# Windowed attention and a gated MLP on one core: order from a list scheduler, one stock of PSUM banks, casting loads for batches 0 and 1, DMA transposes for the later q and k

## Chip, cores, metric

One core of one Trainium2 chip. The metric is device time in microseconds (us) of one execution, median of several. "Span" is the profiled part of it, some 1.7 us shorter. TensorE is PE, VectorE DVE, ScalarE ACT, GpSimd POOL, SyncE SP in the profile. SBUF and PSUM are the memories that the kernels place their tiles in; every matmul of both kernels writes to one of PSUM's banks. The DMAs of the program are issued by GpSimd or SP, and the profile shows what the core's DMA engines move; a DMA has landed when its data is there.

## The reference

```python
# q, k, v: [8 batches, 8 heads, 576, 64]; float32
rel = pos[:, None] - pos[None, :]
plain   = (rel >= 0) & (rel < 32)                       # heads 0 to 3
dilated = (rel >= 0) & (rel < 128) & (rel % 4 == 0)     # heads 4 to 7
attn = softmax(where(mask, q @ k.T / 8, -1e9)) @ v
x = attn.transpose(0, 2, 1, 3).reshape(4608, 512)
h = x @ w_in                                            # [512, 2048]
out = (h * sigmoid(beta * h)) @ w_out                   # [2048, 512]
```

The MLP runs in nine tiles of 512 tokens, each with 16 groups of h (four matmuls of 512 columns each). Attention of one batch (576 tokens) is spread between the MLP's matmuls of the tile before.

## The kernel before

Its order is written by hand, and each engine carries out its own queue in that order (in the trace GpSimd's cast of batch 0's v at 23.0 us, then the loads of w_in from 25.0). Three pools share eight PSUM banks (2 + 1 + 5). q and k of the plain heads are loaded as float32, cast on an engine and transposed on TensorE; those of the dilated heads are cast into DRAM and loaded by DMA transposes.

```python
psum_h = psum("psum_h", 2)
psum_o = psum("psum_o", 1)
psum_at = psum("psum_at", 5)
# ...
cast_v(0, 1, G)                # G is GpSimd: waits for batch 0's v
for g in range(4):
    load_w_in(g)               # DMAs issued on GpSimd's queue, behind that cast
load_qk(1, "k")
load_qk(1, "q")
load_vd(1)
for name in STEPS_FIRST:       # "K0 Q0 K1 S00 Q1 ...": a fixed list of attention steps
    # ...
    attention_step(0, name)
for kind, hp in (("k", 0), ("q", 0), ("k", 1), ("q", 1)):
    cast_qk(1, kind, hp, G)
for g in range(4):
    load_w_out(g)
load_vp(1)
# ...
for t in range(NTT):           # then h and o groups of tile t, attention steps dealt between them
```

The softmax here doesn't subtract the row's maximum and nothing guards it: scores larger than these inputs give would overflow.

## Time and profile before

| | before |
|---|---|
| time, median (range) | 364.0 us (362.6 to 364.74, 4 runs) |
| span of the profiled run, mean granted clock | 364.4 us, 0.983 |
| first MLP matmul | 36.75 us |
| wait for batch 2's transposed q | 76 to 86 us |
| steady period | 36.0 us |

The prediction below quotes the views. The row of the granted TensorE clock, in tenths, 40 slices of the span:

```profile
PEclk9999999999996999999999999999999999999998
```

Only one slice (109 to 118 us, at 6 tenths) is well below full clock. The packed trace's first clock record in this run is at 41.6 us, and before it the row shows full clock, though the 512-column matmuls from 36.75 to 41.7 us start 0.427 us apart, for 0.216 from 150 us on: there the spacing of the matmuls is the surer sign.

A milestone that I use is the start of VectorE's gate, the instruction that writes g: there are 16 per tile (32 for tile 0 in the changed kernel, which cuts that tile in two), so a steady period is the time from one gate to the sixteenth after it. For the kernel before that is 258.5 - 222.5 = 36.0 us.

### The profile page before, as it was taken

The numbers are of one execution on the slowest core, as the hardware profiler recorded it, in microseconds if no ns is written. First come the engines' busy times: TensorE is split into PE (matmuls) and PEld (weight loads), VectorE is DVE, ScalarE is ACT, GpSimd is POOL, SyncE is SP. The second block draws the span as 40 slices with busy tenths as digits, with TensorE's granted clock in tenths as the row PEclk, the third lists the DMA queues.
The fourth block names the chain that finished last, engine by engine and source line by source line (L and its number), as shares of the span: only waits on it lengthen the run. The fifth ranks groups of instructions, "written<-read, shape, count | busy, mean of one in ns | idle before, by whom it ended". The sixth has DMA issues, their size and how long they took to land.

```text
span 364.4 us, 6201 instructions
## 1 busy us (share of the span) xinstructions
PE 315.1 (86%) x2305; PEld 167.3 (46%) x2305; DVE 205.2 (56%) x440; ACT 197.1 (54%) x380; POOL 149.8 (41%) x204
## 2 busy tenths in 40 slices
PE   0266999885977999989999999899989999999995
PEld 0254455442443555545554545454545444444442
DVE  6477488556641966485648565756576635334400
ACT  1373486354651776567656755575657545435511
POOL 8444740364285438453936493549243200000000
PEclk9999999999996999999999999999999999999998
DMA  7999999898937950983099419831101110111032
GB/s 180 167 242 210 221 205 149 216 219 216 221 76 188 232 81 23 215 222 78 29 220 250 93 33 233 221 82 30 31 29 31 29 31 29 42 47 29 29 75 72
DMA packets 66751, 45.77 MB, mean 126 GB/s; under 512 B 45968, under 2 KB 57248, under 8 KB 66464
## 3 DMA queue, kind: packets, MB, share of 16 engines
q1 hardware_dynamic: 55728, 35.67, 40.8%
q0 software_dynamic: 10992, 9.70, 17.0%
q8 instruction: 18, 0.29, 0.4%
q14 instruction: 13, 0.11, 0.1%
HBM read 40.89 MB, written 14.16 MB: 151 GB/s over the span
## 4 chain that ended last, share of the span: by engine, by line
PE 67%; DMA 10%; DVE 7%; POOL 6%; ACT 4%; issue 3%; SPq 2%; POOLq 0%; ACTq 0%
PE o_ps L376 28%; PE h_ps L345 26%; DMA w_in_bf<-in_moe_w_in_dram 3%; POOL pt L292 3%; DVE qzd L199 3%; PE at L345 3%; DMA qdT<-qd 3%; PE at L306 3%; SPq L192 2%; PE at L288 2%; DMA vd_st<-in_v_dram 2%; DVE g L353 2%; PE h_ps L376 2%; PE at L322 2%; POOL qb L206 2%
## 5 line engine op out<-in xcount | busy, mean ns | idle before, releaser
L353 DVE SCALAR_TENSOR_TENSOR g<-tnh,h_ps 128x512 bf16<-128x512 bf16 x134 | 91.3, 686 | 105.6 <-ACT tnh L350 105.2
L345 PE MATMUL h_ps<-xT,w_in_bf 128*128 128x512 bf16 x536 | 138.4, 384 | 12.0 <-DVE g L353 9.7
L376 PE MATMUL o_ps<-w_out_bf,g 128*128 128x512 bf16 x544 | 139.2, 384 | 2.9 <-ACT osb L381 2.9
L350 ACT ACTIVATE tnh<-h_ps,beta_half 128x512 bf16<-128x512 f32 x134 | 92.1, 687 | 69.6 <-PE h_ps L345 67.2
L345 PEld LDWEIGHTS <-w_in_bf 128*128 128x128 bf16 x576 | 52.7, 99 | 60.4 <-issue 15.7
L376 PEld LDWEIGHTS <-g 128*128 128x128 bf16 x576 | 52.6, 99 | 53.0 <-issue 6.1
L290 ACT ACTIVATE pt<-at 128x288 bf16<-128x288 f32 (+1 forms) x112 | 47.2, 443 | 11.9 <-PE at L288 11.9
L292 POOL TENSOR_TENSOR pt<-pt,mask_d 128x288 bf16<-128x288 bf16 x48 | 34.9, 727 | 41.0 <-ACT pt L290 35.1
L313 DVE TENSOR_TENSOR xs<-at,rcp 72x256 bf16<-72x256 f32 (+1 forms) x96 | 44.6, 465 | 3.3
L306 PEld LDWEIGHTS <-pt 128*128 128x128 bf16 x448 | 26.3, 103 | 20.4 <-POOL pt L292 8.0
L381 ACT ACTIVATE osb<-o_ps 128x512 f32<-128x512 f32 x34 | 20.3, 597 | 27.2 <-PE o_ps L376 27.2
L292 POOL TENSOR_TENSOR pt<-pt,mask_PP 128x384 bf16<-128x384 bf16 x24 | 22.3, 936 | 21.5 <-ACT pt L290 21.4
L332 ACT COPY xT<-at 128x288 bf16<-128x288 bf16 x32 | 12.7, 397 | 26.0 <-PE at L322 26.0
L322 PE MATMUL at<-ident_b,xs 72*128 72x72 bf16 (+1 forms) x224 | 21.6, 209 | 5.7 <-DVE xs L313 5.7
L292 POOL TENSOR_TENSOR pt<-pt,mask_FP 128x384 bf16<-128x384 bf16 x12 | 12.0, 998 | 35.2 <-ACT pt L290 35.2
L309 DVE RECIPROCAL rcp<-at 72x4 f32<-72x4 f32 (+1 forms) x96 | 17.1, 178 | 15.6 <-PE at L306 14.8
L306 PE MATMUL at<-vd,pt 128*128 128x65 bf16 x256 | 19.9, 201 | 6.8 <-POOL pt L292 6.8
L206 POOL CAST kb<-k_st 72x512 bf16<-72x512 f32 x28 | 16.3, 610 | 17.9 <-PE at L306 17.9
L322 PEld LDWEIGHTS <-xs 72*128 72x128 bf16 (+1 forms) x224 | 15.5, 101 | 17.2 <-DVE xs L313 7.7
L239 POOL CAST vd<-vd_st 128x2048 bf16<-128x2048 f32 x8 | 15.3, 1914 | 10.5 <-DMA vd_st<-in_v_dram 10.5
L288 PE MATMUL at<-qzd,kdT 128*128 128x144 bf16 x128 | 18.6, 238 | 0.7 <-DVE qzd L199 0.7
L206 POOL CAST qb<-q_st 72x512 bf16<-72x512 f32 x28 | 16.3, 610 | 4.8 <-DMA q_st<-in_q_dram 4.8
(64 smaller groups left out, 229.0 us busy)
## 6 DMA issues: line engine op xcount, KB each, us to landing
vp_st<-in_v_dram SPq DMA_DIRECT2D x24, 192.0 KB, 6.7
vd_st<-in_v_dram SPq DMA_DIRECT2D x8, 512.0 KB
k_st<-in_k_dram SPq DMA_DIRECT2D x6, 576.0 KB
q_st<-in_q_dram SPq DMA_DIRECT2D x6, 576.0 KB
vd_st<-in_v_dram SPq DMA_DIRECT2D x8, 384.0 KB
kd<-in_k_dram POOLq DMA_DIRECT2D x8, 288.0 KB, 7.7
qd<-in_q_dram POOLq DMA_DIRECT2D x8, 288.0 KB, 8.7
w_in_bf<-in_moe_w_in_dram POOLq DMA_DIRECT2D x4, 512.0 KB, 16.1
```

The lines of the kernel that those rows point to most:

```text
L206: (eng.copy if eng is nc.scalar else eng.tensor_copy)(out=qkb[b, kind][:, hp, :, h2, :], in_=stage[b, kind][:, 2 * hp + h2].rearrange("p ( ...
L288: nc.tensor.matmul(sc[:, a, 0:2 * n], lhsT=lhsT, rhs=rhs, start=True, stop=True)
L290: nc.scalar.activation(out=w, in_=sc[:, :, 0:2 * n], func=ACT.Exp, scale=SCALE)
L292: eng.tensor_tensor(out=w, in0=w, in1=mask, op=ALU.mult)
L306: nc.tensor.matmul(pv[:, a, h2, :], lhsT=pt[x][:, c:c + P], rhs=rhs, start=True, stop=True)
L313: nc.vector.tensor_tensor(out=xs_t[b, x, jx][:, a0:a0 + m], in0=pv[0:n, :, :, 0:D], in1=rcp[0:n, 0:m].unsqueeze(3).to_broadcast([n, m, 2, ...
L322: nc.tensor.transpose(xp[:, a * n:(a + 1) * n], xs[:, a].rearrange("p h d -> p (h d)"), ident_b[0:n, 0:n])
L345: nc.tensor.matmul(hps, lhsT=w_in_bf[:, kt, fb * P:(fb + 1) * P], rhs=xT[:, kt, t * NTOK:(t + 1) * NTOK], start=(kt == 0), stop=(kt == NKT ...
L350: nc.scalar.activation(out=tnh[:], in_=hps, func=ACT.Tanh, scale=beta_half[:, fb:fb + 1])
L353: nc.vector.scalar_tensor_tensor(out=g[:], in0=tnh[:], scalar=1.0, in1=hps, op0=ALU.add, op1=ALU.mult)
L376: nc.tensor.matmul(ops[:], lhsT=g_t[t, fb][:, tb * P:(tb + 1) * P], rhs=w_out_bf[:, fb, :], start=(fb == 0), stop=(fb == NFB - 1))
L381: nc.scalar.mul(out=osb[:], in_=ops[:], mul=0.5)
```

## The change

The intent: let a scheduler with estimated durations place every instruction, give all uses one stock of banks, start the MLP sooner, and take q/k transposes off TensorE from batch 2 on. The diff is long; its core, cut:

```diff
-    psum_h = psum("psum_h", 2)
-    psum_o = psum("psum_o", 1)
-    psum_at = psum("psum_at", 5)
+    BANKS = [psum_pool.tile([P, 512], FP32, name=f"bank{i}") for i in range(8)]
+    plan = Plan(range(8))                 # CAPS = {"h": 3, "o": 2, "a": 8}
...
-STEPS = ("K0 Q0 K1 Q1 S00 S01 ...").split()
+class Plan:                               # picks, again and again, the ready instruction that can
+    def run(self, filler=None, ...):      # start first, then by its place in the order (vt)
...
+    def direct_qk(b, z, h0, deps, vt):    # batches 0 and 1: casting load, token-major
+        src = (k, q)[z][b, h0:h0 + 4].rearrange("h (t T) d -> t h (T d)", T=R)
+        return load("POOL", ((ks, qs)[z][:, h0:h0 + 4], src), deps, vt, 576, .38)
+    def cast(b, z, h0, deps, vt): ...     # batches 2 to 7: cast into DRAM on GpSimd's queue,
+    def crossbar(b, z, h0, deps, vt): ... # then a DMA transpose on SP's, for all heads
...
+    def t_masks3(e):                      # late fills, one entry of GpSimd's queue
+        for n in ("FP", "PP"):
+            nc.gpsimd.tensor_copy(out=mask_e[n]..., in_=mask_p[n]...)
+        nc.gpsimd.memset(kz[:], 0.0)
+        nc.gpsimd.memset(qzd[1][64:128, 0], 0.0)
+        nc.gpsimd.memset(qzd[1][0:64, 1], 0.0)
...
-            nc.sync.dma_start(out=dst, in_=osb[a:a + n])     # rows scattered
+                nc.sync.dma_start(out=out[r0:r0 + P, cols], in_=ob[:, cols])
```

## The prediction

> **What bounds the kernel now.** I read the page's slices first, then the chain that ended last, then the instructions in order of time at the start and in one steady batch, then busy times by stretch.
>
> Slices of 9.1 us each (busy tenths):
>
> ```profile
> PE   0266999885977999989999999899989999999995
> DMA  7999999898937950983099419831101110111032
> ```
>
> The DMA row is full for ten slices (91 us) and falls off afterwards; the matmul row is full from the fifth slice on, with holes at slices 8 to 13. So there are two stages: a start bound by transfers, then a long stage bound by TensorE. The chain that ended last, from 0 to 40 us:
>
> ```profile
> 1.31 5.62 DMA kd<-in_k_dram
> 6.95 2.84 SPq L192
> 9.84 4.56 SPq L192
> 15.08 7.78 DMA vd_st<-in_v_dram
> 23.02 1.97 POOL vd L239
> 24.99 11.71 DMA w_in_bf<-in_moe_w_in_dram
> 36.75 1.89 PE h_ps L345 x4
> ```
>
> The first MLP matmul waits for w_in, and w_in is late because its issue stands on GpSimd's queue behind the cast of vd, which waits for a load that stands behind two DMA transposes on SP's queue. It is a serial chain of issues, not lack of bandwidth. The four matmuls from 36.75 start 0.42 us apart (38.43 - 36.75 over 4), against 0.215 later, so TensorE also starts at half speed, until 41.7: 12 matmuls, 2.5 us lost. One steady batch, in order of time:
>
> ```profile
> 249.93 1.03 PE L345 MATMUL h_ps<-xT,w_in_bf 128*128 128x512 bf16 x4
> 250.79 0.29 PE L288 MATMUL at<-qzd,kdT 128*128 128x144 bf16 x2
> 250.92 1.03 PE L376 MATMUL o_ps<-w_out_bf,g 128*128 128x512 bf16 x4
> ...
> 257.59 0.42 PE L253 MATMUL at<-ident_b,kb 72*128 72x72 bf16 x8
> 257.85 1.03 PE L345 MATMUL h_ps<-xT,w_in_bf 128*128 128x512 bf16 x4
> ...
> 267.14 0.38 PE L345 MATMUL h_ps<-xT,w_in_bf 128*128 128x512 bf16 x1 [1.45 <-DVE g L353]
> ```
>
> Starts, not durations, give the cost: four 512-column matmuls take 0.86 us (250.79 - 249.93), two 144-column ones 0.13, eight 72-column transposes 0.26. All fit columns/2.4 ns plus 2.5 ns. The last line is one of the two waits of the period (h has only two banks and waits for VectorE's gate). From 231.18 to 267.14 is 35.96 us; the work in it is 128 MLP matmuls x 0.216 = 27.6, and 5.8 of attention (1.04 q/k transposes, 2.0 scores, 1.7 values, 1.05 back transposes), 33.5 in all, so 2.5 us are waits. Adding the starts up the same way over the whole trace from 36.75 to the last matmul at 359.9: 288.4 us of work and 34.6 of excess: 3 before 60 us, 17.5 from 60 to 120, 14 after. The largest wait is
>
> ```profile
> 76.01 9.78 DMA qdT<-qd
> ```
>
> batch 2's transposed q, at 76 to 86 us.
>
> [...] the granted clock is 0.84 from 86 to 118 us, just after the long wait.[...] In the stretch 42 to 53 us, where only the casting weight loads run, the trace shows 206 GB/s written as bf16, which is 412 GB/s of float32 read.[...]
>
> **The change, part by part.**
>
> *TensorE's work.* From the changed kernel's instruction order: 15 filler matmuls ahead of everything and 20 in batch 0's attention, and q/k transposes for batches 0 and 1 alone. For batches 2 to 7 that removes 32 x 0.0325 = 1.04 us each, 6.2 in all. Plain scores become 24 matmuls of 96 columns for 12 of 192: the same columns, +0.03 us. The first tile is cut into 288 + 224 tokens, same columns. From its first MLP matmul on, I sum 284.3 us of work (288.4 before).
>
> *Steady batches.* Work per period falls to 33.5 - 1.0 = 32.5. Three banks for h and a common stock should end the 1.45 us wait, and masks spread over two engines the 0.7 us wait for GpSimd. ScalarE loses qz copies, GpSimd the q/k casts (56 x 0.61 = 34 us in all); VectorE gains spreads of q and k and most masks. Summing VectorE's list at the durations of the page (gate 0.69 x 16, norm 12 x 0.64, ten masks x 0.36, five or so spreads and copies x 0.6, some xT copies) gives 27 us of a 33 us period: 80%, so some waits remain. I take 1 us of waits per period: 33.5 for 35.96.
>
> *The start.* GpSimd's order is now four q/k loads, identity, vd, masks (4.9 us in the trace), fills (two memsets of 1024 elements, about 1.2 us each by the 0.33 to 0.6 of 288, 3 in all), five vp loads (0.83 each), w_in, w_out. So w_in is issued at about 17.5, not 25. The first packet follows a GpSimd issue by 3.1 us (1.31 to 4.4; 25.0 to 28.1). Transfers then queue at 412 GB/s read:
> - q/k of batch 0, 4 x 0.59 MB[...]: 4.4 to 12; vd to 14; vp, small rows, to about 20.
> - w_in 4.2 MB: 20.6 to 30.8 (its third and largest part last). w_out to 41.
> - batch 1's q/k to 48.7, vd to 51, vp to about 56.
> - batch 2's four casts and its v loads (1.6 MB) share the engines from about 50 to 65. Four DMA transposes follow on SP's queue (issues took 1.3 to 4.7 us each, median 2.2): the last lands near 72, and the spreads of q take 2 to 3 us more.
>
> TensorE follows: batch 0's attention ends near 24, h(0) starts at 24 for 36.75 but stands for w_in's last part until about 31; batch 1's attention waits for q/k (43 to 49) and v (56), ends near 65. The order puts h(1)'s first 28 matmuls (6 us) and two o groups next, then batch 2's scores. Its first plain scores can start at about 75. From that instruction on, 249.1 us of TensorE work remain.
>
> Sum: 75 + 249.1 + 2 (batch 2's exp, mask, value chain) + 5 (waits in the following periods) + 4.5 (from the last matmul to the end, as now: 359.9 to 364.4) = 335.6. The store at the end is halved and goes out in one piece, 0.5 to 1 us less: **334 us**, 8.3% faster. Cross-check: batch 2's input is ready at 75 instead of 86.5 (11.5 gained), 90 to 118 us held 10 us of excess of which I give back half (5), and five periods x 2.4 = 12: 28.5, or 336.
>
> **The rivals.**
>
> *Transfers stay the bound longer.* Four transposes per batch for two, behind casts written to DRAM and read back; all four must land before plain scores. For: SP's queue is in order and its transposes blocked it 4.6 us at the start. Against: at 200 to 250 us the DMA engines are busy half the time or less (0.30 to 0.57 of the stretch). Steady periods would be safe; the start could slip to 82 or 85 and give 342 to 346.
>
> *VectorE becomes the bound* in the steady stage: 27 us of 33[...]; in-order queues made ahead from estimates. If each period stayed at 35.5, the gain would be the start's alone: 345.
>
> *The start goes as the scheduler intends.* If v loads leave early, [...] transposes take their shortest 1.3 us, the plain scores of batch 2 could start at 65 to 68, and waits vanish: 322 to 326.
>
> *It gains nothing:* wrong order somewhere makes TensorE stand for tens of us[...].[...] I see no place for 20 us of loss.
>
> **Range and chances.** The start's uncertainty is about -9 to +9 us around 75, the steady stage's -4 to +8. Together 322 to 345 for 8 in 10. A 2% gain needs under 357; that leaves 23 us of room, so faster 0.95, same 0.04, slower 0.01.
>
> **What would show it right or wrong.** Right: first MLP matmul at 22 to 26 us and a wait for w_in just after; batch 1's attention with TensorE below half busy between 41 and 65; plain scores of batch 2 from 70 to 80, ended by a DMA transpose or a spread; periods of 33 to 34 us after that, with no wait of h for the gate above 1 us; no q/k transposes after batch 1; DMA full until about 70. Wrong: periods of 35 or more with VectorE above 90% (second rival), transposes landing after 85 or TensorE waiting for raw or dq in later batches (first rival), or the excess in the first 75 us under 35 us (third).

## The result, and the profile after

The changed kernel took 348.6 us in the median (347.01 to 351.17, 4 runs): 4.1% faster, ratio 0.9594 (95% interval 0.9541 to 0.9647). It is faster, but outside the predicted range of 322 to 345. Ratios here are the mean time of one kernel's fast runs over that of the other's of the same rounds, so not quite the ratio of the medians quoted. Executions over 1.5% slower than the fastest of the same kernel are left out of the means. Measured again, on chip 13 (e10 below), it took 348.88 us, ratio 0.9542.

| | predicted | measured |
|---|---|---|
| first MLP matmul | 24 us | 26.5 |
| first h group of 512 columns (tile 1) | 65 us | 75.7 |
| batch 2's last DMA transpose of q and k landed | 72 us | 74.9 |
| batch 2's q and k spread in SBUF | 75 us | 85.5 |
| batch 2's first plain scores on TensorE | 75 us | 87.5 |
| steady period | 33.5 us | 32.4 |
| time | 334 us | 348.6 |

The first MLP matmul, the landing of batch 2's q and k and the steady period were about right or better. What came late is what stands between the landed data and TensorE. ("Spread": copied from where a transpose lands to the rows from which the scores read.) The slices of the changed kernel, 8.7 us each, show where TensorE lost time:

```profile
PE   6859955879996999999999999999999999999995
PEclk9987996858998799999999999999999999999999
DMA  6999997940899799169918962995010100110021
```

TensorE is half busy in slices 6 and 7 (44 to 61 us), and the granted clock is 0.50 from 53.8 to 60.6 and from 67.4 to 81.1 us, in slices 7 to 10, where the kernel before has 1.00 (52 to 86 us). TensorE's instructions in order of time (start, duration, what; in brackets the idle time before and what ended it):

```profile
26.54 2.11 PE L668 MATMUL bank<-xT,w_in_bf 128*128 128x288 bf16 x8
...
54.21 0.64 PE L540 MATMUL bank<-qzd,dk 128*128 128x144 bf16 x4 [4.36 <-POOL qzd L314]
57.23 0.66 PE L386 MATMUL bank<-ident_b,g 72*128 72x72 bf16 x8 [2.39 <-POOL g L197]
...
75.70 6.25 PE L668 MATMUL bank<-xT,w_in_bf 128*128 128x512 bf16 x16 [0.49 <-ACT xT L197]
...
87.49 1.24 PE L551 MATMUL bank<-qd,kz 128*128 128x96 bf16 x16 [0.22 <-ACT pt L576]
...
112.77 0.40 PE L540 MATMUL bank<-qzd,dk 128*128 128x144 bf16 x2 [3.48 <-DVE g L680]
```

The two long waits of batch 1's attention end with GpSimd: a memset (L314, a late fill) and a relay (L197, the copy that regroups k and q). So here is GpSimd's own queue over that time:

```profile
32.46 0.77 POOL L320 DMA_DIRECT2D raw<-in_v_dram  x1 [3.33 <-DVE g L680]
37.44 0.83 POOL L320 DMA_DIRECT2D vp<-in_v_dram  x1 [4.22 <-DMA w_out_bf<-in_moe_w_out_dram]
42.76 0.82 POOL L320 DMA_DIRECT2D vp<-in_v_dram  x1 [4.49 <-DMA w_out_bf<-in_moe_w_out_dram]
45.28 0.82 POOL L320 DMA_DIRECT2D vp<-in_v_dram  x1 [1.70 <-DMA st<-in_k_dram]
47.76 0.82 POOL L320 DMA_DIRECT2D vp<-in_v_dram  x1 [1.67 <-DMA st<-in_q_dram]
...
52.93 1.22 POOL L314 MEMSET qzd<- 64x1152 bf16 x1
...
56.12 2.12 POOL L197 COPY g<-st 72x1024 bf16<-72x1024 bf16 x2
```

The four loads of batch 1's plain v need nothing from w_out or from k and q; their destination is free. What they wait for is their turn: in this trace GpSimd's DMAs use eight semaphores (99 to 106) in rotation, and each of the four loads was issued 0.28 or 0.29 us after the DMA eight places ahead of it, the last with its semaphore, had landed (at 37.16, 42.47, 44.99 and 47.48). Four loads that cost 0.82 us each to issue thus hold the queue for 12.1 us (4.22 + 4.49 + 1.70 + 1.67). The load before them (first line) waits 3.33 us more. The view names a gate, but that load's semaphore (104) is the one of w_in's third load, which landed at 31.91 us, 0.55 us before the issue: most of this wait is for its turn too. So the fills, batch 2's casts and the relays behind them run at 48.6 to 58.2. In the scheduler's own plan the fills stood at 27.5 to 32.5 us and the relays at 43.8 to 46.3; its model has no such turn.

The delay goes on through VectorE's queue. Batch 2's last transpose landed at 74.9 us. GpSimd made its half of the spreads by 78.1, but VectorE's half stands behind gates of tile 1, which wait for tile 1's late h:

```profile
82.52 0.46 DVE L197 COPY qzd<-dq 64x1152 bf16<-64x1152 bf16 x1
...
83.73 0.81 DVE L197 COPY kz<-raw 64x1152 bf16<-64x1152 bf16 x1
84.57 0.92 DVE L197 COPY qd<-raw 64x1152 bf16<-64x1152 bf16 x2
```

In the plan VectorE's spreads stood at 66.6 to 71.4 us. So batch 2's plain scores (87.49) could not have started before 85.5.

The stop at 109 to 113 us is named as a wait for the gate (3.48). That gate stood on VectorE's queue behind two spreads of batch 3's q, and these waited for a DMA transpose. The chain that ended last, then VectorE:

```profile
98.69 5.71 DMA st<-in_v_dram
104.41 5.45 DMA raw<-s
```

```profile
109.95 1.96 DVE L197 COPY qd<-raw 64x1152 bf16<-64x1152 bf16 x2 [3.60 <-DMA raw<-s]
111.94 0.69 DVE L680 SCALAR_TENSOR_TENSOR g<-tnh,bank 128x512 bf16<-128x512 bf16 x1
```

Batch 3's last transpose lands at 109.9. Its casts were issued at 88.1 to 90.1, behind two masks of batch 2 that GpSimd holds for late scores, and the last of them landed at 98.0; the transpose was issued 6.4 us after that, behind another transpose and four loads of v on SP's queue. Ahead of the masks GpSimd stood still for 8.2 us:

```profile
86.31 0.73 POOL L589 TENSOR_TENSOR pt<-pt,mask_d 128x288 bf16<-128x288 bf16 x1 [8.22 <-issue]
87.43 0.73 POOL L589 TENSOR_TENSOR pt<-pt,mask_d 128x288 bf16<-128x288 bf16 x1 [0.39 <-ACT pt L576]
88.10 0.54 POOL L320 DMA_DIRECT2D s<-in_k_dram  x1
```

The steady stage, on the other hand, has hardly any waits left. Busy time by stretch, 150 to 310 us (TensorE, weight loads, VectorE, ScalarE, GpSimd, granted clock, DMA share, GB/s), first the kernel before:

```profile
150.00:310.00 160.00, 152.14 (x1168) 81.39 (x1167) 98.04 (x195) 98.65 (x190) 70.81 (x90) 1.00 0.41 102
```

and the changed one:

```profile
150.00:310.00 160.00, 160.00 (x1147) 82.79 (x1146) 113.47 (x251) 93.82 (x175) 36.88 (x42) 1.00 0.54 109
```

TensorE is busy all 160 us and VectorE 71%. From 120 us on, the spacing of TensorE's starts leaves 0.7 us of waits in all, where the kernel before had 14.

### The profile page after: what moved, and what is told of

Read it like the earlier page. It is cut to its first block, busy times and chain, and to the rows that moved or that the text cites.

```text
span 349.5 us, 6333 instructions
## 1 busy us (share of the span) xinstructions
PE 320.6 (92%) x2348; PEld 174.7 (50%) x2348; DVE 229.8 (66%) x517; ACT 189.8 (54%) x367; POOL 121.1 (35%) x153
## 2 busy tenths in 40 slices
DMA packets 73422, 42.03 MB, mean 120 GB/s; under 512 B 55712, under 2 KB 68016, under 8 KB 73008
## 4 chain that ended last, share of the span: by engine, by line
PE 74%; DMA 9%; POOL 9%; DVE 3%; issue 2%; ACT 2%; SPq 1%; POOLq 0%; ACTq 0%; DVEq 0%
PE bank L695 33%; PE bank L668 31%; DMA st<-in_q_dram 6%; PE bank L609 3%; PE bank L636 2%; PE bank L540 2%; DMA st<-in_v_dram 2%; DMA raw<-s 2%; PE bank L551 1%; POOL vp L320 1%; POOL st L320 1%; POOL pt L589 1%; DVE qd L197 1%; DVE xs L622 1%; ACT pt L576 1%
## 5 line engine op out<-in xcount | busy, mean ns | idle before, releaser
L675 ACT ACTIVATE tnh<-bank,beta_half 128x512 bf16<-128x512 f32 (+2 forms) x160 | 102.5, 645 | 97.0 <-PE bank L668 95.1
L668 PE MATMUL bank<-xT,w_in_bf 128*128 128x512 bf16 (+2 forms) x640 | 153.5, 370 | 1.8 <-DVE g L680 0.8
L680 DVE SCALAR_TENSOR_TENSOR g<-tnh,bank 128x512 bf16<-128x512 bf16 (+2 forms) x160 | 100.6, 632 | 72.8 <-ACT tnh L675 71.2
L695 PE MATMUL bank<-w_out_bf,g 128*128 128x512 bf16 x576 | 147.0, 382 | 0.0
L576 ACT ACTIVATE pt<-bank 128x288 bf16<-128x288 f32 (+1 forms) x112 | 44.7, 447 | 14.2 <-PE bank L540 11.0
L622 DVE TENSOR_TENSOR xs<-bank,rcp 72x256 bf16<-72x256 f32 (+1 forms) x96 | 44.6, 465 | 3.3
L609 PEld LDWEIGHTS <-pt 128*128 128x128 bf16 x448 | 23.6, 101 | 15.9 <-issue 2.7
L713 ACT ACTIVATE osb<-bank 128x512 f32<-128x512 f32 (+1 forms) x36 | 21.3, 593 | 15.6 <-PE bank L695 14.5
L197 ACT COPY xT<-bank 128x288 bf16<-128x288 bf16 x41 | 16.0, 397 | 14.2 <-PE bank L636 13.9
L636 PE MATMUL bank<-ident_b,xs 72*128 72x72 bf16 (+1 forms) x224 | 19.8, 212 | 2.2 <-DVE xs L622 2.2
L589 DVE TENSOR_TENSOR pt<-pt,mask_d 128x288 bf16<-128x288 bf16 x36 | 16.9, 490 | 4.8 <-ACT pt L576 4.3
L609 PE MATMUL bank<-vd,pt 128*128 128x65 bf16 x256 | 17.0, 199 | 2.9 <-POOL pt L589 1.6
L197 POOL CAST vd<-st 80x1024 bf16<-80x1024 f32 (+1 forms) x12 | 12.6, 1059 | 5.5 <-DMA st<-in_v_dram 3.6
L197 POOL COPY kz<-raw 64x1152 bf16<-64x1152 bf16 x7 | 10.8, 1546 | 8.4 <-DMA raw<-s 8.3
L197 DVE COPY xT<-bank 128x288 bf16<-128x288 bf16 x23 | 10.3, 450 | 3.7 <-PE bank L636 3.4
```

Source lines behind the costliest of these rows:

```text
L197: (nc.scalar.copy if e == "ACT" else E[e].tensor_copy)(out=out, in_=in_)
L576: nc.scalar.activation(out=pt_of(x, j, n).rearrange("p (a b) n -> p a b n", a=2), in_=sc[:, :, 0:2 * n].rearrange("p a (b n) -> p a b n", ...
L589: E[e].tensor_tensor(out=w, in0=w, in1=m, op=ALU.mult)
L609: nc.tensor.matmul(pv[:, a, h2, :], lhsT=pt[x][:, c], rhs=rhs, start=True, stop=True)
L622: nc.vector.tensor_tensor(out=xs[x, jx][:, a0:a0 + m], in0=pv[0:n, :, :, 0:D], in1=rc[0:n, 0:m].unsqueeze(3).to_broadcast([n, m, 2, D]), o ...
L636: nc.tensor.transpose(xp[:, a * n:(a + 1) * n], xs[x, j][:, a].rearrange("p h d -> p (h d)"), ident_b[0:n, 0:n])
```

## The experiments

**Theory A:** the missing 14 us went to GpSimd's in-order queue, in two places (behind the loads' turn at 33 to 58 us, behind the masks at 80 to 90), with some half clock beside the stops. **Rival B:** the transfers and batch 2's own chain set the time, whatever GpSimd does (my first rival of the prediction; its number, 342 to 346, lay nearest). Then, for the part that went better than predicted, **theory A2**: h's banks end the steady waits; **rival C**: the scheduler's order does it.

Twelve kernels ran in three jobs (e1 to e4; b1, b2, e5 and e6; e7 to e10), each on a chip of its own beside the kernel before. All gave the correct result. In e1 to e4 and e6, TensorE, ScalarE and SP carry out the same instructions in the same order as the changed kernel.

| | edit | median us | ratio to before (95%) |
|---|---|---|---|
| e10_after | changed kernel again | 348.88 | 0.9542 (0.9469 to 0.9615) |
| e1_fill | late fills on VectorE | 344.34 | 0.9449 (0.9408 to 0.949) |
| e2_fill_relay | and relays of batch 1 | 343.53 | 0.9356 (0.9267 to 0.9446) |
| e3_casts | two masks off GpSimd | 344.64 | 0.9473 (0.9428 to 0.9517) |
| e4_both | e2 and e3 | 337.36 | 0.9267 (0.9213 to 0.9322) |
| e6_vp | v's four loads ahead of w_out | 343.82 | 0.9461 (0.9358 to 0.9565) |
| e8_e4vp | e4 and e6 | 340.6 | 0.9304 (0.9213 to 0.9395) |
| e9_fill | e4, fillers until 26 us | 336.71 | 0.9248 (0.9194 to 0.9302) |
| e5_h2 | changed kernel, two banks for h | 344.43 | 0.9459 (0.9375 to 0.9543) |
| e7_direct | changed kernel, no DMA transposes | 362.19 | 0.9915 (0.9855 to 0.9976) |
| b1_h3 | before, three banks for h | 357.92 | 0.9843 (0.9752 to 0.9933) |
| b2_win | before, w_in issued sooner | 372.35 | 1.0239 (1.0133 to 1.0344) |

In two jobs the kernel before spread over 361 to 370 us, with two or three of its seven runs slow. The changed kernel itself gave 0.9594 in its own job and 0.9542 as e10; gains below are taken from the first and are 1.9 us smaller from the second. The times themselves are clearer: no run of e1, e3, e4 or e6 took longer than 345.74 us, and none of the changed kernel's eight took less than 346.12.

### e1, e2: what stands behind the loads, moved off the queue

```diff
-            nc.gpsimd.tensor_copy(out=mask_e[n]..., in_=mask_p[n]...)
-        nc.gpsimd.memset(kz[:], 0.0)            # and the two of qzd[1]
+            nc.vector.tensor_copy(out=mask_e[n]..., in_=mask_p[n]...)
+        nc.vector.memset(kz[:], 0.0)
```

> The changed kernel with the late fills (two mask copies, zeros of kz and of the second qzd) emitted for VectorE instead of GpSimd; order on TensorE, ScalarE and SP unchanged. Theory A (GpSimd's in-order queue sets batch 1: its last vp issue is held to 47.8 us, then 5.5 us of fills stand before the casts and the two copies of k and q): TensorE's wait of 4.4 us before batch 1's dilated scores falls below 1, the copies on GpSimd start near 50.6 instead of 56.1, h of the second tile starts near 71 instead of 75.7, and the time falls by 4 to 6 us. Rival B (batch 1 waits for transfers or for its own chain of exp, mask and values): h of the second tile starts within 1 us of 75.7 and the time within 1.5 us.

For e2 also:

```diff
-                        copy(e, rl[:, z, i], (ks, qs)[z][...])
+                        copy("DVE" if b == 1 else e, rl[:, z, i], (ks, qs)[z][...])
```

> As e1_fill, and the two copies of batch 1's k and q that GpSimd makes (behind the casts) go to VectorE too, same place in its order. Theory A: the transposes that waited for them run near 50 instead of 57.2, h of the second tile starts near 68, 6 to 9 us less than the changed kernel. Rival B: as the changed kernel within 1.5 us, the wait moving to v of batch 1, whose last load is issued at 47.8.

e1: tile 1's h starts at 70.95 instead of 75.70, and the ratio falls by 0.0145 from the changed kernel's 0.9594, 5.3 us. e2: by 0.0238, 8.7 us, but two of its four runs were slow (the profiled one too, 347.47 us at clock 0.94), so this rests on two runs, 342.7 and 338.82. Both lie where theory A put them. In e1 the 4.4 us wait for the fill is gone.

### e3: batch 3's casts issued sooner

```diff
-                E[e].tensor_tensor(out=w, in0=w, in1=m, op=ALU.mult)
+                E[early(b, e)].tensor_tensor(out=w, in0=w, in1=m, op=ALU.mult)
# cut: early() sends the first two masks of batch 2 that were on GpSimd to VectorE
```

> The changed kernel with two of batch 2's masks moved from GpSimd to VectorE, so that the casts of batch 3, which stand behind them in GpSimd's queue, can be issued at about 78 instead of 88 us; all else in order. Theory A: batch 3's last DMA transpose lands near 99 instead of 109, TensorE's 3.6 us wait there goes and with it the half-clock window after it (2.7 us lost): 5 to 6.5 us less. Rival B (the transposes are bound by transfers, or by the stores ahead of them on SP's queue): less than 1.5 us.

The casts are issued at 78.6 instead of 88.1, and the stop at 109 us is gone. The 5 to 6.5 us expected count 2.7 for the half clock from 111.8 to 118.6 us; that it goes with the stop was my estimate. The gain is 0.0121, 4.4 us (2.5 against e10): less than the 5 to 6.5 expected, and about the size of the stop (3.5). Batch 3's last transpose landed at 103.2, not 99; that was soon enough.

### e4: both

> e2_fill_relay and e3_casts together. Theory A: the gains add, 11 to 15 us less than the changed kernel, 334 to 338 us. Rival B: within 2 us of it. Rival C (half clock is the larger part): the gain is over 15 us because TensorE no longer falls to half clock between 54 and 81 us, or, if it still does, under 8.

337.36 us: the gains of e2 and e3 (8.7 + 4.4 = 13.1) nearly add up (0.0327, 11.9). TensorE and GpSimd in e4's profile, in order of time, at the places shown above:

```profile
52.96 0.43 PE L386 MATMUL bank<-ident_b,g 72*128 72x72 bf16 x8 [1.46 <-DVE g L197]
...
68.88 3.61 PE L668 MATMUL bank<-xT,w_in_bf 128*128 128x512 bf16 x15 [0.49 <-ACT xT L197]
...
78.04 1.24 PE L551 MATMUL bank<-qd,kz 128*128 128x96 bf16 x16 [0.23 <-DVE g L680]
```

```profile
42.78 0.82 POOL L320 DMA_DIRECT2D vp<-in_v_dram  x1 [4.36 <-DMA w_out_bf<-in_moe_w_out_dram]
...
48.77 0.54 POOL L320 DMA_DIRECT2D s<-in_k_dram  x1 [1.36 <-DMA st<-in_k_dram]
...
73.50 0.54 POOL L320 DMA_DIRECT2D s<-in_k_dram  x1
```

The loads still wait their turn (4.36), but nothing that TensorE needs soon stands behind them. Batch 2's scores come at 78.04 instead of 87.49, and the clock's mean is 0.985 instead of 0.951. VectorE's spreads of batch 2 end at 76.4 instead of 85.5. The same transfers and the same DMA transposes, and 11 us less: rival B falls.

### e6, e8: the loads' turn itself

```diff
+    def w_out_and_vp1(n):            # emitted where w_out's loads were
+        if n == 0:
+            for h4 in range(4):
+                dma("POOL", vp[1][:, :, h4, 0:D], plain_v(1, h4))
+        dma("POOL", w_out_bf[:, 8 * n:8 * n + 8, :], ...)
# cut: the four loads' own places in the plan stay, and issue nothing
```

> The changed kernel with batch 1's four loads of plain v issued ahead of the two of w_out on GpSimd's queue, every other instruction of every engine in the same order. Theory A, first half (each GpSimd DMA waits for the one eight earlier, so these four stand for w_out and hold up all that follows on GpSimd): they are issued at about 21 to 24 us instead of 37.4 to 47.8, the masks and fills run at 33 to 40 instead of 48.6 to 54.1, the 4.36 us wait for qzd goes, and the relays start as batch 1's k and q land, near 47 to 50. w_out lands 3 to 5 us later. First h of 512 columns at 69 to 72 instead of 75.7; 342 to 345 us (ratio 0.938 to 0.946). Rival B (the queue is not the point, the transfers are): with w_out later and the same bytes, no gain: 347 to 351 us.

Nothing but the place of four loads in one queue is changed. GpSimd in e6's profile:

```profile
20.30 3.32 POOL L320 DMA_DIRECT2D vp<-in_v_dram  x4
...
36.75 0.53 POOL L309 COPY maske_FP<-mask_FP 128x384 bf16<-128x384 bf16 x1
...
45.76 0.52 POOL L320 DMA_DIRECT2D s<-in_q_dram  x1 [3.26 <-DMA w_out_bf<-in_moe_w_out_dram]
```

The loads go out at 20.3 with no wait, and the fills come 12 us sooner (36.75 for 48.57). The fills are still on GpSimd here, so this gain does not come from VectorE, where they are shorter (1.07 us for kz in e9, 2.14 on GpSimd). The last line is the best evidence for the turn: now it is a cast of batch 2, the eighth DMA after the second load of w_out, that waits for w_out, with which it has nothing to do. The time is as theory A said (343.82; expected 342 to 345). Tile 1's h starts at 69.08. The new order has a price that I had not expected: batch 0's masks now stand behind the four loads and a wait of w_out's second load for its turn (0.75 us). TensorE waits 5.62 us for a mask, where the changed kernel waited 1.58, and the first MLP matmul comes at 30.16 instead of 26.54.

> The best so far (late fills and relays on VectorE, two masks of batch 2 moved so that batch 3's casts go early) with batch 1's loads of plain v ahead of w_out as well. Theory A says that with fills and relays off GpSimd's queue, hardly anything on the path stands behind those four loads any more, so the two cures are for the same wait and do not add: 335 to 339 us, within 2 us of 337.4. Were the loads' turn a wait of its own, it would be 3 us or more faster (331 to 334).

e8 is not faster than e4 (0.9304 against 0.9267, intervals overlap; median outside what I expected by 1.6 us). That is what cures for the same wait would do. But e8 pays e6's price as well: TensorE waits 4.34 us for batch 0's masks, and the first MLP matmul comes at 29.8 instead of e4's 26.2. So that the cures would not add without it is not shown.

### e9: the half clock at the start

```diff
-    plan.run(filler, 15000.0)
+    plan.run(filler, 26000.0)
```

> The best so far with filler matmuls allowed until 26 us of the plan instead of 15 (20 more of them, in gaps of batch 0's attention). If half clock at 23 to 30 us[...] goes and up to 3 us of it, 334 to 337 us and a mean clock of 0.99 or more. If fillers come too late[...]: 337 to 340 and the clock as before (0.985).

In e9's profile the granted clock stays up through slices 3 and 4, where e4's row begins 9987:

```profile
PEclk9999799979999999999999999999999999999999
```

In this pair of profiles the clock is higher where the fillers were added (9 tenths in slices 3 and 4, for 8 and 7); but e9's slices 5 and 9 are at 7, where e4's are at 8 and 9, and over all runs the mean clocks overlap (e4 0.972 to 0.985, e9 0.975 to 0.989), so that fillers hold the clock is not shown. The time is 336.71, the ratio 0.0019 below e4's: not told apart. The next stop is 2.76 us, at 30.8 to 33.5, for a gate on VectorE, which is busy with the late fills then; e4 has the same stop (2.65).

How much the half clock costs can be counted in the traces. After 50 us the changed kernel ran at half clock (granted 0.50) from 53.8 to 60.6, 67.4 to 81.1 and 111.8 to 118.6 us. Its matmuls of 512 columns start 0.427 us apart there and 0.216 from 150 to 200 us, those of 72 columns 0.060 and 0.032: columns/1.2 ns and columns/2.4 ns + 2.5 ns fit these. Counted so, the matmuls in the three stretches lost about 8 us; in e10 (half clock at 55.0 to 61.8 and 68.7 to 78.9) they lost 4.6, and e4's trace has no half clock after 36.6. So by my estimate up to 5 to 8 of e4's 11 us can be the clock, less where a wait would have taken its place. The mean clock of a run is a poorer measure: e6 took 340.68 us at 0.985 and 343.66 to 345.21 at 0.960 to 0.968, but fast runs of the kernel before took 363.36 and 366.22 us, both at 0.988.

### b1, e5: where the steady gain comes from

```diff
-    psum_h = psum("psum_h", 2)      # b1: the kernel before
+    psum_h = psum("psum_h", 3)
-    psum_at = psum("psum_at", 5)
+    psum_at = psum("psum_at", 4)
```

> The kernel before with one bank moved: three PSUM banks for h, four for attention (two and five before). Theory A (the wait of 1.45 us per period for the gate is a matter of h's two banks, so the gain of the steady stage comes from the banks): seven periods with 1.45 us less, some of it given back by attention's four banks, so 5 to 8 us faster (0.978 to 0.986). Rival C (the steady gain comes from the order that the list scheduler makes, banks alone do nothing): under 2 us, or slower because attention then waits for its four banks.

b1 is 1.6% faster, 5.7 us. The totals of TensorE's waits say why: before,

```profile
PE h_ps L345 <- DVE g L353: 9.7, 8, 2.9
```

and in b1:

```profile
PE h_ps L345 <- DVE g L353: 1.3, 2, 0.9
```

(us in total, times, longest). Its period is 252.2 - 217.9 = 34.3 us, 1.7 less than before. All four runs (357.22 to 359.6) are below the fast ones of the kernel before in that job (361.44 to 366.67).

```diff
-    CAPS = {"h": 3, "o": 2, "a": 8}  # e5: the changed kernel
+    CAPS = {"h": 2, "o": 2, "a": 8}
```

> The changed kernel with the scheduler allowed two banks for h instead of three, which re-plans the order. Theory A (the banks of h give the steady stage its missing waits): the wait for the gate comes back, 1 to 1.5 us per period, 6 to 10 us slower than the changed kernel (time about 355 to 359). Rival C (the order does it: the scheduler puts attention's work between h groups so that two banks are enough): within 3 us of the changed kernel (346 to 352).

Theory A2 fails here: with two banks the re-planned kernel's period is 205.4 - 172.9 = 32.5, as with three (32.4), and it is not slower in all (344.43; the intervals of e5 and e10 overlap). Other periods of e5 are 33.6 to 33.8, but the two waits there (1.17 and 1.00 us) are for VectorE's normalization, and e10 has one such as well (0.97); after tile 0 the wait for h's gate does not come back. In the hand-made order the third bank is worth 5.7 us; in the scheduler's order it is not needed. e5's plan differs at the start too, so its 4 us there are not evidence for anything about banks.

### e7: the DMA transposes undone

```diff
-    DIRECT = 2
+    DIRECT = B                       # all batches by casting loads and TensorE transposes
-    rl = g_t[1][0:RT, 0:8]...        # the relay's space, shared with g
+    rl = const([RT, 4096], BF16, "rl")[:]...
# cut: a small kz, and when the loads of batches 2 to 7 may start
```

> The changed kernel with one part undone: q and k of batches 2 to 7 also come by casting loads and are transposed on TensorE, as batches 0 and 1 are (its own tile for the relay, zeros only where still used; the scheduler re-plans). TensorE gets back 32 transposes per batch, 6.2 us in all. If the DMA transposes pay what the prediction said, a steady period goes from 32.4 to 33.4 or 33.5 us and the time is 5 to 7 us over the changed kernel (352 to 356). If the round trip through DRAM and the four transposes hold batch 2 up at the start by more than that (first rival of the prediction), it is as fast or faster (340 to 348). If ScalarE and VectorE, which get back the copies out of PSUM, become the bound, periods are 35 or more and the time over 360.

13.3 us slower than the changed kernel in the same rounds, which is more than expected, and the fault is in my count: e7 has 512 TensorE transposes for 128, so 64 more per batch, not 32 (before, the dilated half came by DMA already). 384 x 0.0325 = 12.5 us. The start is no better for it: tile 1's first gate comes at 78.6 us, and at 78.5 in the changed kernel. The period is 238.4 - 202.3 = 36.1 us, 3.7 more than 32.4: 2.1 are the transposes (64 x 0.0325), the rest is not split further. The marks of my third case (periods of 35 or more, over 360 us) were met too, but not its cause: from 150 to 310 us VectorE was busy 118.1 and ScalarE 103.9 of the 160 us.

### b2: w_in issued sooner in the kernel before

```diff
-    cast_v(0, 1, G)
     for g in range(4):
         load_w_in(g)
+    cast_v(0, 1, G)
```

> The kernel before with w_in's four loads issued ahead of GpSimd's cast of batch 0's v, nothing else. w_in should then be issued at about 13.5 us instead of 25.0 and land by about 28. TensorE's own attention of batch 0 lasts to 34.7, so the first h comes at 34.7 to 35.5 instead of 36.75. Theory A (the later start is bound by the issues on GpSimd's queue and by batch 2's data, not by w_in): 1 to 3 us faster, the long wait for batch 2's transposed q keeps most of its place (74 to 78 us). Rival (w_in's issue is what held the whole start): 8 us or more faster.

Neither was right: it is 2.4% slower. GpSimd and TensorE in b2's profile:

```profile
13.08 3.01 POOL L161 DMA_DIRECT2D w_in_bf<-in_moe_w_in_dram  x4
28.07 1.89 POOL L239 CAST vd<-vd_st 128x2048 bf16<-128x2048 f32 x1 [11.99 <-DMA vd_st<-in_v_dram]
```

w_in is issued 12 us sooner, but batch 0's v then lands at 28.1 instead of 23.0; the first MLP matmul comes at 38.35 instead of 36.75. SP's queue shows more of the loss: beside w_in's transfers its next two DMA transposes take 10.01 and 6.76 us to issue, for 4.69 and 2.47 before, and batch 1's k and q behind them are issued from 33.0 us on instead of 23.6. By tile 1's first gate the kernel is 6.7 us behind (83.7 for 77.0), at the end 5. The DMA engines moved 201 GB/s from 13 to 28 us, and in the kernel before 199 from 13 to 25: the earlier issue moved no more, it only took from others. How much of that is bandwidth and how much SP's queue is not separated.

## Why the prediction was wrong

**Right, by its own steps.** TensorE's work (284 us from the first MLP matmul) and the cost of columns/2.4 ns + 2.5 ns (measured from 150 to 200 us: 0.216 us at 512 columns, 0.0625 at 144, 0.0425 at 96); w_in issued at 18.1 (said 17.5); first MLP matmul 26.5 (said 22 to 26); batch 2's last transpose landed at 74.9 (said 72); no q/k transposes after batch 1; 249.1 us of work from batch 2's first plain scores to the end. VectorE didn't become the bound, so the second rival fell. Batch 0's q and k landed at 6.6, 8.6, 10.8 and 12.9 us (said: all by 12, an estimate).

**The step that failed** is "batch 1's attention waits for q/k (43 to 49) and v (56), ends near 65", with "the spreads of q take 2 to 3 us more" and "Its first plain scores can start at about 75" built on it. It took the landing of data, and the length of the copies, as what TensorE waits for. Batch 1's data landed in time (k and q by 49.5, v by 53.7). But the relays, fills and masks between data and TensorE stood on GpSimd's queue, which my working stopped following after the issue of w_out. In its place: the loads of v waited 12.1 us for their turn, the fills and relays came at 48.6 to 58.2 and tile 1's h at 75.7 (+10.7); behind tile 1's gates on VectorE's queue, batch 2's spreads ended at 85.5 (+10.5), and its plain scores came at 87.5 (+12.5). The sum with the measured term: 87.5 + 249.1 + 4.5 = 341.1, and 8.4 of waits and half clock to the span's 349.5, where I had 7 less 0.75. That these are near is luck: mine were for batch 2's chain and steady waits, the 8.4 are nearly all before 120 us, the stop at 109 and the half clock after it among them. The same in-order queue, with batch 3's casts behind batch 2's masks, made that stop (e3: 4.4 us). My sum was also of spans, and a time is 1.7 us longer than its span.

e4 removes both and takes 337.4, e9 336.7: within the predicted range, 3 us over its middle. So the prediction described a kernel in which GpSimd's queue holds up nothing that TensorE needs soon.

**Too pessimistic:** 1 us of waits per steady period; there was none. Of the 3.6 us by which the period fell, 1.04 is the transposes removed and up to 1.7 what a third bank gives the old order; 0.8 or so is left to the order. e5 shows that the scheduler needs no third bank, so this split holds for the old kernel as a start only.

**Half right:** "It is a serial chain of issues, not lack of bandwidth" at the start. b2 breaks the chain and loses, with no more bytes moved per us. The changed kernel's sooner start is therefore not explained by issue order alone; that it also moves less (42.03 MB in the whole kernel for 45.77) fits, but no run shows it separately.

**Also too loose:** half clock "just after the long wait". The long wait was the transposed q's; TensorE itself stood still for 2.88 us at most there (85.4 to 88.3), and ran at half clock from 89.4 to 92.8. In the changed kernel the half clock at 67.4 follows 6.8 us at full clock in which no wait was over 0.6 us. So these traces give no length of stop that brings half clock about.

**Still open:** how much of e4's 11 us is the clock. My estimate from the spacing of matmuls is up to 5 to 8 us; no run holds the stops and changes the clock alone, and what brings the half clock about is not shown.

## What to carry to other kernels

Follow every engine's queue, VectorE's and SP's too, and the DMA-issuing one first, up to the moment where the bound engine needs it: an instruction that nobody waits for can hold those that are waited for (here four loads held GpSimd's queue for 12.1 us). Put long waits for memory and small urgent work on different queues, and tell a scheduler what a queue of DMAs really waits for (here the landing of the DMA eight places ahead, 0.28 or 0.29 us before each of the four issues). Before an issue is moved ahead, look whether it will only take from the transfers it joins (b2 moved 201 GB/s, the kernel before 199, and b2 was 2.4% slower).
